# A fused attention and two MLPs: three blocks of tokens instead of two go uncombined through the first MLP, one weight matrix at a time

## The chip, the cores and the metric

The kernel runs on one core of a Trainium2 chip. The metric is the device time of one execution, in microseconds; of the kernel before three runs gave 1757.72, 1759.16 and 1761.06, median 1759.16. TensorE (PE) multiplies, VectorE (DVE) and ScalarE (ACT) do the elementwise work, and all transfers between DRAM and the on-chip memory are issued, in order, by SyncE (SP).

## The reference

```python
# q, k, v: (8, 8, 576, 64)
q_s = softmax of q over its last axis;  k_s = softmax of k over the sequence
kv = einsum('bhsd,bhse->bhde', k_s, v)
x  = einsum('bhsd,bhde->bhse', q_s, kv)      # -> (4608, 512)
h = x @ w_in                                 # (512, 2048)
r = maximum(h, 0);  x = (r * r) @ w_out      # (2048, 512)
gate = 1 / (1 + exp(-(x @ w_gate)))          # (512, 1536)
val = x @ w_val
return (gate * val) @ w_out2                 # (1536, 512)
```

The weights of both MLPs arrive as 64-bit floats.

## The kernel before

The 4608 tokens are nine blocks of 512 (0 to 8), four key tiles of 128 channels each. Every float32 product is made of three matmuls on high and low parts (`mm3`, L217 to 220: high by high, high by low, low by high), so everything that is multiplied is first split: ACT makes the high part (`hi_of`, L212), DVE subtracts it for the low part (`lo_of`, L215).

A raw weight tile is 128 x 512 numbers of 64 bits. `w_load` (L245) fetches it; ACT takes the words apart (L255, L261), DVE makes a 32-bit float of them in four instructions (L268, L269, L272, L279). The split of it, `whl`, is 0.5 MB, is written to a DRAM tensor (`w_store`, L297) and fetched again by later stages (`w_fetch`, L302, into `ws`).

Most stages use a Strassen-Winograd scheme with seven products in place of eight ("combined"). It needs sums of weight tiles (`w_comb`, L293) and of input tiles, and works on a pair of blocks; PE then multiplies 128 x 512 tiles. Four units of 84 matmuls make the first matrix of the first MLP for a pair; its second matrix takes 384 matmuls more, uncombined. The ninth block has no partner, so its two halves of 256 tokens are paired (`in_stage` with `nt` 256): the same 720 matmuls, with 256 columns each.

Blocks 0 and 1 go through the first MLP uncombined (`conv_stage`), 384 matmuls of 512 columns each: for each of 16 slices f of the hidden layer, 12 matmuls for the first matrix (`c_in`) into bank 4 or 5, relu and square on ACT (`c_g`), the split of that (`c_hi`, `c_lo`, tile `g0hl`), and 12 matmuls for the second matrix (`c_out`) into banks 0 to 3. In block 0 the weights are converted as they are needed, both matrices side by side, and the four sums of each group of the first matrix are made and split in the same stretch: 8 splits for each 4 raw tiles. Block 1 fetches the splits back. Then come the pairs (2, 3) and (4, 5) through the first MLP, (0, 1) and (2, 3) through the second, (6, 7) and the single block 8 through the first, and the rest through the second. The attention of later blocks is spread beside these stages.

The order of the instructions is set by `Plan`: every operation has a due time, engines it may run on, predecessors, and buffers it takes and gives back by tag. A list scheduler with fixed costs plays this through once and emits each engine's program in the order in which it would start. `plan.chain` forces an order on the weight fetches. On the chip only that order and the semaphores remain, and every engine, SP included, takes its instructions strictly in turn. Buffers are few: 10 of tag W (raw tiles, fetched splits), 14 of X, 19 of f, 5 of w.

Of the kernel before, what the change touches and what calls it, by code (L numbers as in the profile page):

```python
# [26 lines left out]
CHOSEN = object()  # L27
# [118 lines left out]
def attention_mlp_mlp(  # L146
# [158 lines left out]
    def plan_w(kind, g, T, dT, tag, conv, lead=6.0):  # L305

        N4 = [(kind, g, b) for b in range(4)]
        for b in range(4):
            t = conv[b] - 8 if conv else T + b * dT
            key = N4[b]  # L310
            add(t - lead, {DMA: 1.5}, ("wl",) + key, w_load, kind, g, b, tag, take=["W", tag] if wide else [tag])
            if wide:
                add(t, {ACT: 0.66}, ("wa",) + key, w_abs, key, tag, after=[("wl",) + key])
                add(t + 0.1, {ACT: 0.66}, ("wc",) + key, w_low, key, after=[("wl",) + key])
                add(t + 0.2, {DVE: (1.55, 2.05)}, ("wb",) + key, w_bits, key, after=[("wa",) + key])
                add(t + 0.4, ROUND, ("wr",) + key, w_round, key, CHOSEN, after=[("wb",) + key, ("wc",) + key], give=["W"])
        done = "wr" if wide else "wl"
        U = 4 * dT if not conv else 1.0
        t1 = (max(conv) - 4 if conv else T + U)

        def split(i, b, t, after, give=(), keep=None, store=True):
            key = (kind, g, i)
            htag = "X" if keep else "W"
            add(t, {ACT: 0.63}, ("wh",) + key, w_hi, key, b, htag, after=after, take=[htag])
            add(t + 0.2, LOW, ("wo",) + key, w_lo, key, b, CHOSEN, after=[("wh",) + key], give=give)
            if store:
                add(t + 1 if keep else t - 10, {DMA: 1.5}, ("ws",) + key, w_store, key, after=[("wo",) + key], give=[] if keep else ["W"])

        def comb(nm, o, a, b, op, t, after):
            add(t, VEC, ("wm", kind, g, nm), w_comb, kind, g, o, a, b, op, CHOSEN, after=after)  # L330

        D_ = [(done,) + x for x in N4]
        s = dT / 2 if not conv else 1.0

        ct = (lambda b: conv[b] - 5) if conv else (lambda b: t1)
        split(4, 3, ct(3), [D_[3]], keep=conv)
        split(1, 0, ct(0), [D_[0]], keep=conv)
        split(2, 1, ct(1), [D_[1]], keep=conv)
        s0 = []
        if conv or kind == "out":  # L340
            split(0, 2, ct(2), [D_[2]], keep=conv)
            s0 = [("wo", kind, g, 0)]
        M = lambda nm: ("wm", kind, g, nm)
        O = lambda i: ("wo", kind, g, i)
        if kind == "out":

            add(t1 + 9, {FREE: 0.0}, ("wfree", kind, g), lambda: None, after=[O(0), O(1), O(2), O(4)], give=[tag] * 4)
            return
        comb("S1", 3, 2, 3, ALU.add, t1 + s, [O(4), D_[2], *s0])
        comb("S3", 2, 0, 2, ALU.subtract, t1 + 2 * s, [M("S1"), D_[0], *s0])  # L350
        comb("S2", 0, 3, 0, ALU.subtract, t1 + 3 * s, [M("S3"), O(1)])
        comb("S4", 1, 1, 0, ALU.subtract, t1 + 4 * s, [M("S2"), O(2)])
        split(5, 3, t1 + 3 * s, [M("S1")])
        split(7, 2, t1 + 4 * s, [M("S3")], give=[tag])
        split(6, 0, t1 + 5 * s, [M("S2")])
        split(3, 1, t1 + 6 * s, [M("S4")], give=[tag])
        add(t1 + 7 * s, {FREE: 0.0}, ("wfree", kind, g), lambda: None, after=[O(5), O(6), O(3)], give=[tag] * 2)

# [90 lines left out]
    NPE = 2  # L449

# [121 lines left out]
    slack = lambda j: SLACK if j > 3 else 0.0  # L572
# [20 lines left out]
    def plan_q(j, p, key, step, qmul):  # L593
# [297 lines left out]
    for g in range(NU):  # L891
        for kind in ("in", "out"):
            plan_w(kind, g, 0, 0, "f", conv_times(kind, g))

    def conv_stage(j, T0, TS):

        ready = lambda kind, g, i: ("wo", kind, g, i) if j == 0 else ("wf", ("c", kind, g, i))
        kvs = [("kv", 0, p) for p in range(NP)]
        tag = "X" if j == 0 else "W"
        for f in range(F1):  # L900
            t = T0 + TS * f
            g, r = divmod(f // 2, 2)
            if j and f % 2 == 0:
                for kind, ii in (("in", ((1, 2), (0, 4))[r]), ("out", ((1, 0), (2, 4))[r])):
                    for i in ii:
                        plan_fetch((kind, g, i), c_use(j, kind, g, i), t - 14 + 3 * (kind == "out"))
            for kt in range(KT):
                i = (1, 2, 0, 4)[2 * r + kt // 2]
                if kt:
                    wait = [("ch", j, f, kt - 1)]  # L910
                elif f > 1:
                    wait = [("cg", j, f - 2)]
                else:
                    wait = kvs if j == 0 else [("cg", j - 1, F1 - 2 + f)]
                add(
                    t, {PE: 3 * MM}, ("ch", j, f, kt), c_in, j, f, kt,
                    after=[("x", j, kt), ready("in", g, i)] + wait, give=["SX"[j]] if f == F1 - 1 else [],
                )
                if f % 2 and kt % 2:
                    add(t, {FREE: 0.0}, ("cf", j, f, kt), lambda: None, after=[("ch", j, f, kt)] + ([("ws", "in", g, i)] if j == 0 else []), give=[tag])  # L920
            add(t + 2.6, {ACT: 1.24}, ("cg", j, f), c_g, f, after=[("ch", j, f, KT - 1)], take=["a"])
            add(t + 3.7, {ACT: 0.62}, ("chi", j, f), c_hi, f, after=[("cg", j, f)], take=["S"])
            add(t + 4.2, LOW, ("clo", j, f), c_lo, f, CHOSEN, after=[("chi", j, f)], give=["a"])
            ii = ((1, 0), (2, 4))[r]
            if f:
                wait = [("co", j, f - 1)]
            else:
                wait = kvs if j == 0 else [("cev", j - 1, o) for o in range(KT)]
            add(t + 6, {PE: 12 * MM}, ("co", j, f), c_out, j, f, after=[("clo", j, f)] + [ready("out", g, i) for i in ii] + wait, give=["S"])
            if f % 2:  # L930
                add(t, {FREE: 0.0}, ("cof", j, f), lambda: None, after=[("co", j, f)] + ([("ws", "out", g, i) for i in ii] if j == 0 else []), give=[tag, tag])
        t = T0 + TS * F1 + 6
        for o in range(KT):
            add(t, {ACT: 0.6} if o % 2 == 0 else {DVE: 0.7}, ("cev", j, o), c_ev, o, after=[("co", j, F1 - 1)], take=["a"])
            add(t + 1, {DMA: 0.8}, ("ost", j, o, 1), c_st, j, o, after=[("cev", j, o)], give=["a"])
        freed[0, 1] = (t + 1, [("cev", j, 0), ("cev", j, 1)])
        freed[2, 3] = (t + 2, [("cev", j, 2), ("cev", j, 3)])
        freed[4, 5] = (t - 4, [("cg", j, F1 - 2), ("cg", j, F1 - 1)])
# [63 lines left out]
    NPAIR = (NB - 1) // 2  # L1002
# [248 lines left out]
```

## Time and profile before

| | |
|---|---|
| median of three runs | 1759.16 us |
| span of the profiled execution | 1754.5 us |
| what lies around the span (median less span) | 4.7 us |
| PE busy | 1683.9 us, 96% |
| DVE, ACT busy | 1151.3 us, 926.1 us |
| moved by DMA | 443.27 MB, mean 253 GB/s |

The profiled execution's own total is not shown; the three runs stand for it. A busy PE is not PE at its peak: the mean granted clock was 0.978 over the span, and well below that in the first two hundred microseconds. A matmul row has the time from start to modelled end; matmuls overlap, so what one costs is the distance between starts.

### The profile page before, as it was taken

How to read it: one execution, taken by the hardware profiler on the slowest of the kernel's cores; microseconds unless marked ns; L12 is line 12 of the kernel's file. 1: busy time of each engine (PE TensorE's matmuls, PEld its weight loads, DVE VectorE, ACT ScalarE, POOL GpSimd, SP SyncE). 2: the span in 40 equal slices, each digit the busy share in tenths (PEclk: the TensorE clock that was granted, in tenths of full speed). 3: DMA queues.
4: the chain of work that ended last, by engine and by line, in shares of the span. 5: the costliest groups of instructions: out<-in, count | busy, mean ns of one | idle time of the engine just before them, and what ended most of it. 6: DMA issues, size and time to landing. Idle time of an engine off the chain costs nothing.

```text
span 1754.5 us, 25121 instructions
## 1 busy us (share of the span) xinstructions
PE 1683.9 (96%) x9124; PEld 1450.3 (83%) x9124; DVE 1151.3 (66%) x2192; ACT 926.1 (53%) x1711; POOL 2.1 (0%) x15
## 2 busy tenths in 40 slices
PE   5877899999989999999999999999999999999999
PEld 4655788788877887889988898888998899889999
DVE  7878877788776577568667685352364485447555
ACT  6776446666646575445457555271453354335344
POOL 0000000000000000000000000000000000000000
PEclk7888899999999999999999999999999999999999
DMA  7778777868778889985766566375777557655797
GB/s 277 269 281 284 257 240 262 308 234 300 266 286 311 315 287 346 346 290 182 248 209 210 177 215 213 105 254 190 287 283 285 192 187 245 204 194 191 226 376 274
DMA packets 149146, 443.27 MB, mean 253 GB/s; under 512 B 15648, under 2 KB 27936, under 8 KB 149024
## 3 DMA queue, kind: packets, MB, share of 16 engines
q1 hardware_dynamic: 149024, 441.68, 72.2%
q8 instruction: 72, 1.18, 0.3%
q14 instruction: 50, 0.41, 0.1%
HBM read 357.20 MB, written 84.41 MB: 252 GB/s over the span
## 4 chain that ended last, share of the span: by engine, by line
PE 79%; DMA 9%; DVE 7%; ACT 3%; issue 1%; SPq 1%; ACTq 0%; DVEq 0%
PE bank L218 25%; PE bank L219 25%; PE bank L220 25%; DMA wraw<-in_moe_w_out_dram 3%; PE xps L550 2%; DMA w_gv<-whl 2%; PE kps L427 1%; DMA w_in<-whl 1%; DMA wraw<-in_moe_w_val_dram 1%; DVE whl L215 1%; DVE wf L279 1%; DVE bX L215 1%; ACT wf L255 1%; DMA wraw<-in_moe_w_gate_dram 1%; DVE wf L272 1%
## 5 line engine op out<-in xcount | busy, mean ns | idle before, releaser
L218 PE MATMUL bank<-bX,ws 128*128 128x512 f32 (+1 forms) x1288 | 480.8, 373 | 8.2 <-DMA ws<-w_in 4.6
L219 PE MATMUL bank<-bX,ws 128*128 128x512 f32 (+1 forms) x1288 | 473.2, 367 | 0.0
L220 PE MATMUL bank<-bX,ws 128*128 128x512 f32 (+1 forms) x1288 | 472.9, 367 | 0.0
L709 DVE TENSOR_TENSOR s<-s,bank 128x512 f32<-128x512 f32 (+1 forms) x303 | 190.0, 632 | 217.8 <-PE bank L220 177.4
L218 PEld LDWEIGHTS bank<-bX,ws 128*128 128x128 f32 x1288 | 244.1, 189 | 48.2 <-DMA ws<-w_in 5.1
L212 ACT ACTIVATE s<-bank 128x512 f32<-128x512 f32 (+1 forms) x303 | 165.7, 554 | 223.2 <-PE bank L220 205.3
L220 PEld LDWEIGHTS bank<-bX,ws 128*128 128x128 f32 x1288 | 243.7, 189 | 40.9
L219 PEld LDWEIGHTS bank<-bX,ws 128*128 128x128 f32 x1288 | 244.1, 190 | 37.2 <-issue 0.5
L212 ACT ACTIVATE bS<-s 128x512 fp32r<-128x512 f32 (+1 forms) x306 | 175.5, 582 | 155.3 <-PE bank L220 136.2
L215 DVE TENSOR_TENSOR bS<-s,bS 128x512 fp32r<-128x512 f32 (+1 forms) x306 | 190.3, 632 | 82.1 <-ACT bS L212 75.1
L218 PE MATMUL bank<-ws,bS 128*128 128x256 f32 x756 | 214.5, 284 | 0.0
L219 PE MATMUL bank<-ws,bS 128*128 128x256 f32 x756 | 213.9, 283 | 0.0
L220 PE MATMUL bank<-ws,bS 128*128 128x256 f32 x756 | 213.9, 283 | 0.0
L218 PE MATMUL bank<-bS,ws 128*128 128x512 f32 (+1 forms) x512 | 188.4, 368 | 1.0 <-DMA ws<-w_out 0.7
L219 PE MATMUL bank<-bS,ws 128*128 128x512 f32 (+1 forms) x512 | 185.9, 363 | 1.4 <-DVE bS L215 1.4
L220 PE MATMUL bank<-bS,ws 128*128 128x512 f32 (+1 forms) x512 | 185.7, 363 | 0.0
L218 PEld LDWEIGHTS bank<-ws,bS 128*128 128x128 f32 x756 | 145.0, 192 | 0.8
L219 PEld LDWEIGHTS bank<-ws,bS 128*128 128x128 f32 x756 | 145.1, 192 | 0.7
L220 PEld LDWEIGHTS bank<-ws,bS 128*128 128x128 f32 x756 | 145.0, 192 | 0.0
L728 ACT ACTIVATE s<-s 128x512 f32<-128x512 f32 (+1 forms) x120 | 70.4, 588 | 130.7 <-DVE s L709 130.6
L218 PEld LDWEIGHTS bank<-bS,ws 128*128 128x128 f32 x512 | 96.7, 189 | 16.9 <-DMA ws<-w_out 1.1
L219 PEld LDWEIGHTS bank<-bS,ws 128*128 128x128 f32 x512 | 96.7, 189 | 16.6 <-DVE bS L215 1.6
(122 smaller groups left out, 2250.0 us busy)
## 6 DMA issues: line engine op xcount, KB each, us to landing
ws<-w_gv SPq DMA_DIRECT2D x210, 512.0 KB, 4.6
ws<-w_out SPq DMA_DIRECT2D x185, 512.0 KB, 4.2
ws<-w_in SPq DMA_DIRECT2D x128, 512.0 KB, 5.3
w_gv<-whl SPq DMA_DIRECT2D x42, 512.0 KB, 5.2
w_out<-whl SPq DMA_DIRECT2D x37, 512.0 KB, 5.2
w_in<-whl SPq DMA_DIRECT2D x32, 512.0 KB, 4.0
wraw<-in_moe_w_out_dram SPq DMA_DIRECT2D x28, 512.0 KB, 4.6
vt<-in_v_dram SPq DMA_DIRECT2D x32, 325.0 KB, 4.9
```

Source lines behind the costliest of these rows:

```text
L212: nc.scalar.activation(out=dst, in_=src, func=AF.Copy)
L215: by_name[engine].tensor_tensor(out=dst, in0=src, in1=hi.bitcast(F32), op=ALU.subtract)
L218: nc.tensor.matmul(ps, ah, bh, start=first, stop=False, skip_group_check=True)
L219: nc.tensor.matmul(ps, ah, bl, start=False, stop=False, skip_group_check=True)
L220: nc.tensor.matmul(ps, al, bh, start=False, stop=last, skip_group_check=True)
L255: nc.scalar.activation(out=t, in_=high.bitcast(F32), func=AF.Abs)
L272: nc.vector.scalar_tensor_tensor(out=w, in0=high, scalar=-0x40000000, in1=w, op0=ALU.bitwise_and, op1=ALU.bitwise_or)
L279: by_name[engine].tensor_tensor(out=w, in0=w, in1=low, op=ALU.add)
L427: nc.tensor.matmul(ps[:, 0:2 * D + 1], kt[:, r, :], vt[:, r, 0:2 * D + 1], start=(r == 0), stop=(r == RK - 1))
L550: nc.tensor.matmul(ps[:, e], kvf[b % 2][p], t[:, e], start=True, stop=True)
L709: nc.vector.tensor_tensor(out=t, in0=t, in1=banks[pr[b]][:, 0:n], op=ALU.add)
L728: nc.scalar.activation(out=t, in_=t, func=AF.Sigmoid)
```

## The change

Three blocks (0, 1, 2) go uncombined, and the pairs of the first MLP become (3, 4), (5, 6), (7, 8). The second MLP keeps its pairs and its half-block stage. The uncombined part is cut by matrix: the first matrix of block 0; then the first of block 1 beside the second of block 0, slice by slice; the first of block 2 beside the second of block 1; the second of block 2. Raw tiles of the first matrix are converted in the first of these stretches, those of the second matrix in the next. All raw tiles now use the 5 buffers of tag w in place of 19 of f, which hold the relu outputs waiting for their second matrix.

The four sums of a group are no longer made beside block 0. Each 32-bit tile of the first matrix is also written to DRAM (`w_store32`, 0.25 MB, 16 of them) and read back in the third stretch or later (`w_load32`), where sums and their splits are made. A tag-w buffer is given back when its split is made and that write has landed. A new chain, `worder`, fixes the order of all raw loads and read-backs.

```diff
+    def w_store32(key):
+        d = dp.tile([128, 512], F32, tag="w32_%s%d%d" % key, name="w32_%s%d%d" % key)
+        nc.sync.dma_start(out=d, in_=wf[key])
+        w32[key] = d
+
+    def w_load32(key, tag):
+        t = wf[key] = tile2(tag, "wf")
+        nc.sync.dma_start(out=t, in_=w32[key])
...
+    def plan_first(kind, g, times, tag):
+        for b in range(4) if kind == "in" else (0, 2, 1, 3):
+            t = times[b]
+            done = plan_raw(kind, g, b, t - 8, tag, 8.0)
+            i = SPLIT[b]
+            plan_split(kind, g, i, b, t - 5, t - 4, done, htag="X")
+            end = [("wo", kind, g, i)]
+            if kind == "in":
+                add(t - 3.9, {DMA: 0.8}, ("w32", kind, g, b), w_store32, (kind, g, b), after=done)
+                end.append(("w32", kind, g, b))
+            add(t - 3, {FREE: 0.0}, ("wfre", kind, g, b), lambda: None, after=end, give=[tag])
+
+    def plan_late(kind, g, T, s, tag):
+        ready = {}
+        for b in range(4):
+            add(T - 8, {DMA: 0.8}, ("wl32", kind, g, b), w_load32, (kind, g, b), tag, after=[("w32", kind, g, b)], take=[tag])
+            worder.append(("wl32", kind, g, b))
+            ready[b] = [("wl32", kind, g, b)]
+        plan_sums(kind, g, ready, {}, T, s, tag)
...
-    T0, TS = 27.0, 6.4
-    TC = F1 * 24 * MM * 1.06
-    T1 = T0 + TS * F1 + 8 + TC
+    T0, TS0, TS1 = 27.0, 4.4, 5.8
+    T2 = T0 + TS0 * F1
+    T3 = T2 + TS1 * F1
+    T4 = T3 + TS1 * F1
+    T1 = T4 + 2.9 * F1 + 4
...
+    for g in range(NU):
+        plan_first("in", g, [T0 + TS0 * (4 * g + 2 * (b // 2)) for b in range(4)], "w")
+    for g in range(NU):
+        plan_first("out", g, [T2 + TS1 * (4 * g + 2 * (b % 2)) + 3 for b in range(4)], "w")
+    for g in range(NU):
+        plan_late("in", g, T3 + 10 + 35 * g, 4.0, "w")
...
-    conv_stage(0, T0, TS)
-    conv_stage(1, T0 + TS * F1 + 1, TC / F1)
+    for f in range(F1):
+        conv_in(0, f, T0 + TS0 * f)
+    for j, T in ((1, T2), (2, T3)):
         for f in range(F1):
+            conv_in(j, f, T + TS1 * f)
+            conv_out(j - 1, f, T + TS1 * f + 3)
+    for f in range(F1):
+        conv_out(NONE - 1, f, T4 + 2.9 * f)
...
-    BLOCKS = [(2 * n, 2 * n + 1) for n in range(NPAIR)] + [(NB - 1,)]
+    IN = [tuple(range(j, j + 2)) for j in range(NONE, NB, 2)]
+    GATE = [(j, j + 1) for j in range(0, NB - 1, 2)] + [(NB - 1,)]
...
-    plan_blocks([1], T0 + 6, TS * F1 - 45)
-    plan_blocks(BLOCKS[1], T0 + TS * F1 - 25, (TC - 20) / 2)
-
-    BESIDE = {0: 2, 3: 3, 4: 4}
+    plan_blocks([1], T0 + 6, TS0 * F1 - 20)
+    plan_blocks([2], T2 + 6, TS1 * F1 - 30)
+    plan_blocks(IN[0], T3 + 5, (T1 - T3 - 40) / 2)
+
+    BESIDE = {0: 1, 3: 2}
...
-    for names in (fetched, xorder, sorder):
+    for names in (worder, fetched, xorder, sorder):
```

DVE, early in block 0, from the second relu output or the third weight tile on; `whl` is a weight split, `g0hl` the split of a relu output, `wf` a 32-bit tile. Before:

```order
L215 TENSOR_TENSOR whl<-wf,whl 128x512
L471 TENSOR_REDUCE qst<-qt 128x8
L417 TENSOR_TENSOR kt<-kt,kps 128x640
L500 TENSOR_SCALAR qst<-qst 128x8
L293 TENSOR_TENSOR wf<-wf 128x512
L215 TENSOR_TENSOR g0hl<-g_446,g0hl 128x512
L293 TENSOR_TENSOR wf<-wf 128x512
L268 TENSOR_SCALAR wf<-wf 128x512
L269 TENSOR_SCALAR wf<-wf 128x512
L272 SCALAR_TENSOR_TENSOR wf<-wraw,wf 128x512
```

In the changed kernel:

```order
L215 TENSOR_TENSOR whl<-wf,whl 128x512 x2
L443 TENSOR_TENSOR kt<-kt,kps 128x640
L530 TENSOR_SCALAR qst<-qst 128x8
L268 TENSOR_SCALAR wf<-wf 128x512
L269 TENSOR_SCALAR wf<-wf 128x512
L272 SCALAR_TENSOR_TENSOR wf<-wraw,wf 128x512
```

The sums (L293) and the splits of relu outputs (`g0hl`) have left this stretch; conversions and their own splits follow each other.

SP, from the first stores of block 0 on; `wraw` is a raw tile, `w_in` and `w_out` as a destination are the DRAM tensors. Before:

```order
L245 DMA wraw<-in_moe_w_in_dram 128x512 x2
L245 DMA wraw<-in_moe_w_out_dram 128x2x256 x2
L297 DMA w_in_384<-whl 128x1024
L297 DMA w_in_398<-whl 128x1024
L245 DMA wraw<-in_moe_w_in_dram 128x512
L459 DMA qt<-in_q_dram 128x512
L297 DMA w_out_435<-whl 128x1024
L245 DMA wraw<-in_moe_w_in_dram 128x512
```

In the changed kernel (L310 is the write of a 32-bit tile):

```order
L310 DMA w_in_336<-wf 128x512
L489 DMA qt<-in_q_dram 128x512
L310 DMA w_in_351<-wf 128x512
L297 DMA w_in_360<-whl 128x1024
L245 DMA wraw<-in_moe_w_in_dram 128x512
L297 DMA w_in_383<-whl 128x1024
L245 DMA wraw<-in_moe_w_in_dram 128x512
L310 DMA w_in_410<-wf 128x512
```

Twelve raw tiles stood ahead of the first store before; now five do, and the sixth and each later raw load stands behind writes of earlier tiles.

## Rows read from the trace of the kernel before

**Rows 1.** The page's slices (40 of 43.9 us): PE busy, granted clock, DMA.
```profile
PE   5877899999989999999999999999999999999999
PEclk7888899999999999999999999999999999999999
DMA  7778777868778889985766566375777557655797
```
**Rows 2.** Windows: length, busy us (instructions) by engine, granted clock, DMA share, GB/s.
```profile
37.80:205.00 167.20, 132.13 (x515) 99.33 (x515) 139.52 (x287) 112.83 (x241) 0.00 (x0) 0.84 0.77 271
37.80:312.00 274.20, 236.45 (x1016) 185.26 (x1016) 220.20 (x465) 170.60 (x345) 0.00 (x0) 0.90 0.77 269
205.00:312.00 107.00, 104.32 (x502) 85.92 (x501) 80.69 (x180) 57.78 (x105) 0.00 (x0) 0.99 0.77 265
312.00:360.00 48.00, 47.30 (x224) 39.11 (x224) 34.40 (x73) 33.80 (x63) 0.00 (x0) 0.99 0.90 312
1221.30:1316.00 94.70, 92.96 (x748) 91.32 (x747) 44.13 (x101) 48.28 (x122) 0.00 (x0) 1.00 0.76 289
1340.00:1400.00 60.00, 60.00 (x266) 49.73 (x265) 29.09 (x44) 21.55 (x36) 0.00 (x0) 1.00 0.63 212
```
**Rows 3.** Timeline of PE: start and end of the uncombined blocks.
```profile
37.86 0.78 PE L218 MATMUL bank<-x,whl 128*128 128x512 f32 x1
...
311.35 0.63 PE L220 MATMUL bank<-g0hl,ws 128*128 128x512 f32 x1
311.78 0.63 PE L218 MATMUL bank<-bX,ws 128*128 128x512 f32 x1
```
**Rows 4.** PE's groups, 880 to 980 us: count, busy, mean ns, idle before.
```profile
L218 PE MATMUL bank<-bX,ws 128*128 128x512 f32 x124 | 51.1, 412 | 0.0
L220 PE MATMUL bank<-bX,ws 128*128 128x512 f32 x125 | 48.9, 391 | 0.0
...
L427 PE MATMUL kps<-vt,kt 128*128 128x129 f32 x50 | 6.5, 276 | 0.0
```
**Rows 5.** DVE's groups, 37.5 to 205 us.
```profile
L215 DVE TENSOR_TENSOR whl<-wf,whl 128x512 fp32r<-128x512 f32 x46 | 30.6, 685 | 13.0 <-ACT whl L212 12.8
L272 DVE SCALAR_TENSOR_TENSOR wf<-wraw,wf 128x512 int32<-128x512 int32 x30 | 20.8, 693 | 1.0
L279 DVE CUSTOM_DVE_ANT_0 wf<-wraw,wf 128x1024 uint16<-128x1024 uint16 x31 | 20.4, 681 | 0.0
L269 DVE TENSOR_SCALAR wf<-wf 128x512 int32<-128x512 int32 x30 | 12.8, 427 | 1.0
L268 DVE TENSOR_SCALAR wf<-wf 128x512 f32<-128x512 f32 x30 | 12.6, 420 | 0.0
L293 DVE TENSOR_TENSOR wf<-wf 128x512 f32<-128x512 f32 x16 | 10.9, 682 | 0.0
```
**Rows 6.** ACT's groups, 37.5 to 205 us.
```profile
L212 ACT ACTIVATE whl<-wf 128x512 fp32r<-128x512 f32 x46 | 27.4, 622 | 26.2 <-DVE wf L279 14.6 <-DMA w_in<-whl 8.4 <-DVE qst L471 3.1
L255 ACT ACTIVATE wf<-wraw 128x512 f32<-128x512 f32 x24 | 15.7, 670 | 10.3 <-DMA wraw<-in_moe_w_out_dram 8.2 <-DMA wraw<-in_moe_w_in_dram 2.0
L510 ACT ACTIVATE qt<-qt,qst 128x64 f32<-128x64 f32 x32 | 8.0, 333 | 1.5 <-DVE qst L500 1.5
```
**Rows 7.** SP's waits, 36 to 205 us: total us, times, longest.
```profile
SPq L297 <- DVE whl L215: 38.5, 27, 4.8
SPq L297 <- DVE wf L268: 18.1, 8, 6.2
```
**Rows 8.** Timeline of DVE: last split of the first MLP's weights.
```profile
209.37 0.69 DVE L215 TENSOR_TENSOR whl<-wf,whl 128x512 fp32r<-128x512 f32 x1 [2.57 <-ACT whl L212]
```
**Rows 9.** Timeline of SP: last weight fetch of block 1.
```profile
292.69 0.32 SPq L302 DMA_DIRECT2D ws<-w_out  x1
```
**Rows 10.** DMA issues, 37.5 to 205 us: count, KB, median us to landing.
```profile
w_in<-whl SPq DMA_DIRECT2D x30, 512.0 KB, 4.0
wraw<-in_moe_w_in_dram SPq DMA_DIRECT2D x10, 512.0 KB, 5.0
```

More of the change, by code (lines that the diff above doesn't have):

```diff
@@ L303, in w_fetch @@
         whl[use] = t
[L305 to L342, printed above, removed]
@@ new lines, in attention_mlp_mlp, with plan_split @@
+    w32 = {}
+    worder = []
+    def w_store32(key):
[5 more added lines that the diff above has]
+        nc.sync.dma_start(out=t, in_=w32[key])
+    def plan_split(kind, g, i, b, t, ts, after, give=(), htag="W"):
+        key = (kind, g, i)
+        add(t, {ACT: 0.63}, ("wh",) + key, w_hi, key, b, htag, after=after, take=[htag])
+        add(t + 0.2, LOW, ("wo",) + key, w_lo, key, b, CHOSEN, after=[("wh",) + key], give=give)
+        add(ts, {DMA: 1.5}, ("ws",) + key, w_store, key, after=[("wo",) + key], give=[] if htag == "X" else ["W"])
@@ new lines, in plan_raw @@
+    def plan_raw(kind, g, b, t, tag, lead):
+        key = (kind, g, b)
+        add(t - lead, {DMA: 1.5}, ("wl",) + key, w_load, kind, g, b, tag, take=["W", tag] if wide else [tag])
+        worder.append(("wl",) + key)
+        if wide:
+            add(t, {ACT: 0.66}, ("wa",) + key, w_abs, key, tag, after=[("wl",) + key])
+            add(t + 0.1, {ACT: 0.66}, ("wc",) + key, w_low, key, after=[("wl",) + key])
+            add(t + 0.2, {DVE: (1.55, 2.05)}, ("wb",) + key, w_bits, key, after=[("wa",) + key])
+            add(t + 0.4, ROUND, ("wr",) + key, w_round, key, CHOSEN, after=[("wb",) + key, ("wc",) + key], give=["W"])
+        return [("wr" if wide else "wl",) + key]
@@ L343, in plan_w, with plan_sums @@
+    def plan_sums(kind, g, ready, own, t, s, tag):
         M = lambda nm: ("wm", kind, g, nm)
         O = lambda i: ("wo", kind, g, i)
[L345 to L357, printed above, removed]
+        def comb(nm, o, a, b, op, t, after):
+            add(t, VEC, M(nm), w_comb, kind, g, o, a, b, op, CHOSEN, after=after)
@@ L449, in attention_mlp_mlp @@
     NPE = 2
+    NONE = 3
+    XTAG = "SXX"
     JACT = 1
@@ L624, in plan_q @@
             kv_users[b, p].append(("xp",) + n)
-        if pe:
-            add(key + 8 * step, {ACT: 0.6}, ("xh",) + n, x_hi, j, p, after=[("xp",) + n], take=["SX"[j]])
+        if j < NONE:
+            add(key + 8 * step, {ACT: 0.6}, ("xh",) + n, x_hi, j, p, after=[("xp",) + n], take=[XTAG[j]])
             add(key + 9 * step, {DVE: 0.7}, ("x",) + n, x_lo, j, p, after=[("xh",) + n], give=["pa"])
@@ L891, in attention_mlp_mlp @@
     for g in range(NU):
[L892 to L899, printed above, removed]
-        for f in range(F1):
[L901 to L938, printed above, removed]
@@ L1081, in gate_stage @@
     def gate_stage(n, t):
-        js = BLOCKS[n]
+        js = GATE[n]
         nt = N if len(js) > 1 else N // 2
@@ L1087, in gate_stage @@
             for kt in range(KT):
-                add(t - 40, {DMA: 0.8}, ("xl", "x2", j, kt), x2_load, j, kt, after=([("ost", j, kt, 1)] if len(js) > 1 else [("ost", j, kt, 1, h) for h in range(2)]) + x_before["gate", n], take=["x"])
+                add(t - 40, {DMA: 0.8}, ("xl", "x2", j, kt), x2_load, j, kt, after=[("ost", j, kt, 1)] + x_before["gate", n], take=["x"])
         xn = ("X2", n)
```

112 lines of the change are left out of this document (86 added, 26 removed).

## Prediction

> **What bounds the kernel now.** I read the slices of the page first. PE is at nine tenths or more in nearly all of them, except the first five, where the granted clock is low as well [rows 1]. So nothing but PE's own work matters later, and the first 200 us are where a change of order can gain. The windows show it. From 37.8 to 205 us PE is busy 132.1 of 167.2 us at a granted clock of 0.84, from 205 to 312 us it is busy 104.3 of 107.0 us at 0.99 [rows 2]. The timeline gives the edges: the first weight matmul starts at 37.86, the last of block 1 ends its turn at 311.78, where the first combined one starts [rows 3].
>
> How much is lost there needs a price for a matmul. From 1340 to 1400 us PE does nothing but 512-column matmuls, 266 in 60 us: 0.2256 us each [rows 2]. Blocks 0 and 1 are 768 of them, 173.3 us. Attention beside them: from 880 to 980 us PE does 374 of these (three lines of 124 to 125) and 50 records of the key-value product [rows 4]; the 374 take 84.4 us, so 15.6 us are attention. A block of 512 tokens brings about one batch, which is 40 such records: 12.5 us. Between 37.8 and 312 us that is three blocks, 37.5 us. Of 274.2 us, 173.3 and 37.5 are work and 63 are lost, to idle time and to a low clock together.
>
> What PE waits for is the conversion of weights. DVE is busy 139.5 of the 167.2 us, 83%, ACT 67%, the DMA engines 77% [rows 2]. The largest groups of DVE are the four steps of a conversion, 0.42 + 0.43 + 0.69 + 0.68 = 2.22 us a tile, the splits at 0.69, and 16 sums [rows 5]. ACT waits 14.6 us of its split time for DVE's last conversion step, 8.4 us for a store that must free a buffer [rows 6], and SP's stores wait 38.5 us for DVE's splits [rows 7]. It is a round of small waits with DVE the fullest.
>
> **The change part by part.** *Matmuls.* The half-block stage goes. From 1221.3 to 1316 us PE ran 748 matmuls, the stage's 720 of 256 columns and 28 others of 512 [rows 2]; less 28 x 0.2256 = 6.3 us it takes 88.4 us. In its place block 2 costs 384 x 0.2256 = 86.6 us. As an exchange of work that is 2 us, nothing more.
>
> *Attention.* Before the end of the uncombined part block 4 now comes too (12.5 us), which stood beside a later stage. It is moved, not saved.
>
> So the new span is 1754.5 - 312.0 - 88.4 - 12.5 + E = 1341.6 + E, where E is the time at which the uncombined part ends. Everything after it has the same stages as before, all bound by PE; I take their seams as unchanged. E without any loss is 37.8 + 1152 x 0.2256 + 4 x 12.5 = 347.7 us. The question is what is lost on top, where 63 us were.
>
> *First stretch (first matrix of block 0).* PE's work is 192 x 0.2256 + 12.5 = 55.8 us; the conversions are slower. DVE has 14 tiles left to convert when the first split is done (31.1 us), 15 splits (10.3 us) and the attention of block 1. For that: busy 139.5, less 108.1 of the six groups of rows 5, less 14 relu splits (9.6), is 21.8 us for one and a half blocks, 15 for one. Rows overlap in a busy time, so this is a lower bound: 56 us or more. ACT has 11 tiles by two steps of 0.67 (14.7), 15 splits of 0.62 (9.3), 64 short exponentials and scalings of 0.333 for block 1 (21.3) [rows 6], and relu and square besides. The end is not before 98 us (60 us, DVE without a gap); at the 83% and 67% these engines reached, and with ACT now nearly as full as DVE, I take 78 us, an end at 116 us.
>
> *Second stretch (block 1's first matrix, block 0's second).* PE: 86.6 + 12.5 = 99.1 us. DVE by difference with the kernel before, which had its last split at 209.4 us [rows 8], 171.6 us after the start: 16 sums (10.9) and 16 splits (11.0) fewer, half a block of attention more (7 at least; I take 10). That gives 160 us, the last split at 198 us, and the two slices of PE that hang on it end at 209. From 116 us PE alone would end at 215; with 6% for waits, 221 us. The extra 16 writes of 0.25 MB lie under other work if the queue has room (below).
>
> *Third and fourth.* 576 x 0.2256 = 129.9 us and two blocks of attention, 25. The sums and their 16 splits (22 us of DVE), 16 read-backs and 16 stores are here, beside PE; conversions are not. Before, with conversions over, PE idled 2.7 of 107 us [rows 2]; I take 6% again, because more bytes go by: 164 us, E = 385.
>
> **Sum.** 1341.6 + 385 = 1726.6 us of span; the median of the runs lies 4.7 above the span shown, so 1731 us. Lost are 385 - 347.7 = 37 us instead of 63.
>
> *The queue.* Counting the transfers in SP's program, block 1's last weight fetch came after 78.2 MB and was issued at 292.7 us [rows 9], 267 GB/s from the start; 19 us later the part ended. Block 2's last fetch comes after 106.0 MB. My E wants it at 366 us, 290 GB/s. From 312 to 360 us the kernel moved 312 GB/s with PE busy 47.3 of 48.0 us [rows 2]. So the rate exists; it is not certain that waits of SP let it through.
>
> **Rivals.**
> (a) *Less is lost.* DVE runs without gaps (98 us) and the later stretches lose 3%: E = 98 + 254 x 1.03 = 360, 1706 us. For it: PE's 2.7 us of idling. Against it: DVE and ACT never ran that full over 60 us. 15%.
>
> (b) *The clock.* PE has 56 us of work in 78 us, with gaps after each pair of tiles. Low clock shows as starts 0.43 us apart, as at 311.35 and 311.78 [rows 3]. If the whole first stretch ran so, 192 x 0.43 = 82.6 us and attention at 1.7 times its price (21) make PE its bound: 104 us, E = 411, 1757 us. The granted clock of 0.84 between 37.8 and 205 us, in which PE idled 35 us, speaks for some of it, not for all. 10%. [...]
>
> (c) *The queue goes no faster than before.* 106.0 MB at 267 GB/s are there at 397 us, E = 416, 1762 us: no gain. Against it: that rate was kept down by waits for DVE [rows 7], which has less to do for each byte of the later stretches. 13%.
>
> (d) *The five buffers: slower.* All 32 raw loads go through five tiles instead of 19. A trip is: landing 5.0 [rows 10], ACT 1.3, DVE 2.2, landing of the 32-bit write 4.0 (as the split's), 12.5 us if nothing waits. 27 tiles follow the first five, so 5.4 trips; they fit into the 160 us of DVE's work up to 30 us a trip. But SP takes its instructions in turn: the load for a freed buffer stands behind the write and the split store of each of the five tiles, and a store's wait for DVE was up to 4.8 to 6.2 us [rows 7]. Five waits of 4.8 make 36.5 us a trip, 197 us, conversions end 37 us late, E = 422 and 1768 us. It decides from a trip of about 35 us on. For it: the sixth raw load stands behind three writes where twelve raw loads stood ahead of any. Against it: the waits are mostly for DVE's progress, which the estimate has already, and are not added five times. 10%. [...]
>
> That the change is not there is no rival: the order shows the stretches as described.
>
> **Numbers.** My forecast has 52%, (a) 15, (b) 10, (c) 13, (d) 10. Range 1708 to 1760: it takes in (b) and most of (a), leaves out (d), half of (c) and the best end of (a), less than 20% together. A measurement tells 0.2% (3.5 us) from no change. Faster than 1755.6: forecast, (a), about half of (b) and the low part of (c), 78%; within: 9%; slower: (d) and the rest of (c), 13%.
>
> **What would show it.** Right: first weight matmul still near 38 us; the last of block 0's first matrix near 116 us; block 1's and block 0's stretch ending near 221 us with DVE fullest until about 200; the first combined matmul near 385 us; no 256-column stage with `bX` before the last stage; later stages unchanged within a few us. Wrong in (b): starts 0.43 us apart through most of the first 80 us. Wrong in (c): DMA share near 0.9 or PE waiting for `ws` after 221 us. Wrong in (d): ACT waiting for raw tiles of 64 bits and DVE idle behind it, while SP waits at L310 or L245. The prediction is wrong as a whole if E is near 385 but the later stages take longer, since I gave them nothing.

## The result, and the profile after

The changed kernel takes 1714.16 us (median of four runs, 1711.9 to 1716.33), the kernel before 1758.61 us beside it (four runs): a ratio of 0.9754, 95% interval 0.9737 to 0.9772. That is 44.5 us less, where 28 were forecast. The profiled execution has a span of 1714.5 us and a time of 1716.33 us.

The page's slices of the changed kernel (42.9 us each; PE busy, granted clock, DMA), to be held against [rows 1]:

```profile
PE   5889999999999999999999999999999999999999
PEclk8989999999999999999999999999999999999999
DMA  6999878799787889799757555755576557655797
```

Two weak slices are left of four after the first. The windows, with the columns of [rows 2], cut where the stretches end; below them one that lies inside the first stretch:

```profile
38.00:117.00 79.00, 68.13 (x283) 50.10 (x284) 66.09 (x147) 67.03 (x160) 0.00 (x0) 0.91 0.92 326
117.00:214.00 97.00, 97.00 (x460) 80.48 (x459) 79.74 (x165) 64.04 (x114) 0.00 (x0) 1.00 0.90 323
214.00:378.00 164.00, 158.79 (x753) 131.06 (x752) 109.75 (x233) 83.22 (x149) 0.00 (x0) 0.99 0.78 271
60.00:80.00 20.00, 16.91 (x77) 11.94 (x77) 18.72 (x44) 19.81 (x51) 0.00 (x0) 1.00 0.94 357
```

In the second stretch DVE still works 82% of the time and converts as before, but PE is busy for all of its 97.00 us. In the first, DVE (84%) and ACT (85%) are both nearly full. The queue carries 326 and 323 GB/s where it carried 271.

The edges, from PE's timeline (start, us, line, operation), as in [rows 3]: the last matmul of the first stretch, the last of the second (of block 0's second matrix), the first combined one, and the last uncombined one.

```profile
116.86 0.39 PE L220 MATMUL bank<-x,whl 128*128 128x512 f32 x1
...
214.34 0.39 PE L220 MATMUL bank<-g0hl,whl 128*128 128x512 f32 x1
...
374.86 0.39 PE L218 MATMUL bank<-bX,ws 128*128 128x512 f32 x1
...
378.72 0.39 PE L220 MATMUL bank<-g0hl,ws 128*128 128x512 f32 x1
```

The ends overlap: six combined matmuls start before the last uncombined one. So that all kernels can be compared, E is from here on the start of the last uncombined matmul, plus its 0.23 us, less 0.2256 us for each combined one ahead of it, and the rest is span less E. The kernel before has E = 314.9 and 1439.6 behind it, the changed kernel 377.6 and 1336.9. To lay them beside each other I give the kernel before a third uncombined block at its price (86.6 + 12.5, so E = 414.0) and take its half-block stage and batch (88.4 + 12.5) off the rest: 1338.7. The 40.0 us between the two spans are then 36.4 in the uncombined part, 1.8 in the exchange of work, and 1.8 in all that follows.

What DVE and ACT do in the first stretch (38 to 117 us; groups as in [rows 5] and [rows 6]):

```profile
L272 DVE SCALAR_TENSOR_TENSOR wf<-wraw,wf 128x512 int32<-128x512 int32 x17 | 11.8, 693 | 0.6
L279 DVE CUSTOM_DVE_ANT_0 wf<-wraw,wf 128x1024 uint16<-128x1024 uint16 x16 | 10.4, 685 | 0.0
L215 DVE TENSOR_TENSOR whl<-wf,whl 128x512 fp32r<-128x512 f32 x15 | 9.8, 682 | 0.6 <-ACT whl L212 0.6
...
L215 DVE TENSOR_TENSOR x<-xps,x 128x512 fp32r<-128x512 f32 x5 | 3.4, 689 | 5.4 <-ACT x L212 5.4
```
```profile
L255 ACT ACTIVATE wf<-wraw 128x512 f32<-128x512 f32 x14 | 8.8, 662 | 4.3 <-DMA wraw<-in_moe_w_in_dram 4.3
L212 ACT ACTIVATE whl<-wf 128x512 fp32r<-128x512 f32 x15 | 8.8, 617 | 0.0
```

The 15 splits cost what they cost before; DVE's wait for ACT ahead of them was 0.6 us, where it had been 12.8 us ahead of 46 splits, and ACT has no idle time ahead of its own. SP's waits in the same stretch (total, times, longest), for [rows 7]:

```profile
SPq L310 <- DVE wf L279: 21.2, 13, 4.3
SPq L297 <- DVE whl L215: 12.6, 9, 4.0
```

The last splits of the first MLP's weights on DVE, for [rows 8], and the last issue of a weight of the second matrix to the uncombined part, for [rows 9]:

```profile
198.28 1.29 DVE L215 TENSOR_TENSOR whl<-wf,whl 128x512 fp32r<-128x512 f32 x2 [1.56 <-ACT whl L212]
```
```profile
364.79 0.32 SPq L302 DMA_DIRECT2D ws<-w_out  x1
```

A store of a split lands 4.3 us after its issue, 4.0 before [rows 10].

### The profile page after: what moved, and what is told of

The parts are those of the page before. It is cut to its first block, busy times and chain, and to the rows that moved or that the text cites. A ratio compares the mean times of both kernels' runs of the same rounds, so it can differ in the third digit from the quotient of the medians.

```text
span 1714.5 us, 24259 instructions
## 1 busy us (share of the span) xinstructions
PE 1666.9 (97%) x8788; PEld 1425.3 (83%) x8788; DVE 1127.2 (66%) x2109; ACT 916.4 (53%) x1649; POOL 2.1 (0%) x15
## 4 chain that ended last, share of the span: by engine, by line
PE 85%; DMA 7%; DVE 4%; ACT 2%; issue 1%; SPq 1%; ACTq 0%; DVEq 0%
PE bank L218 27%; PE bank L220 27%; PE bank L219 27%; PE xps L580 2%; PE kps L453 1%; DMA qt<-in_q_dram 1%; DMA ws<-w_in 1%; DMA wraw<-in_moe_w_gate_dram 1%; DMA wraw<-in_moe_w_out_dram 1%; DMA vt<-in_v_dram 1%; DMA ws<-w_gv 1%; DVE whl L215 0%; PE qsw L511 0%; PE bank L453 0%; ACT wf L255 0%
## 5 line engine op out<-in xcount | busy, mean ns | idle before, releaser
L218 PE MATMUL bank<-bX,ws 128*128 128x512 f32 (+1 forms) x1176 | 446.3, 379 | 7.2 <-DMA ws<-w_in 5.7
L220 PE MATMUL bank<-bX,ws 128*128 128x512 f32 (+1 forms) x1176 | 440.7, 375 | 0.0
L219 PE MATMUL bank<-bX,ws 128*128 128x512 f32 (+1 forms) x1176 | 440.7, 375 | 0.0
L739 DVE TENSOR_TENSOR s<-s,bank 128x512 f32<-128x512 f32 (+1 forms) x279 | 179.9, 651 | 215.4 <-PE bank L220 178.4
L212 ACT ACTIVATE s<-bank 128x512 f32<-128x512 f32 (+1 forms) x279 | 156.7, 568 | 215.4 <-PE bank L220 213.7
L218 PEld LDWEIGHTS bank<-bX,ws 128*128 128x128 f32 x1176 | 222.0, 189 | 47.5 <-DMA ws<-w_in 4.7
L220 PEld LDWEIGHTS bank<-bX,ws 128*128 128x128 f32 x1176 | 221.7, 189 | 40.3
L219 PEld LDWEIGHTS bank<-bX,ws 128*128 128x128 f32 x1176 | 222.1, 189 | 37.7 <-issue 0.5
L212 ACT ACTIVATE bS<-s 128x512 fp32r<-128x512 f32 (+1 forms) x282 | 166.1, 597 | 147.1 <-PE bank L220 129.7
L215 DVE TENSOR_TENSOR bS<-s,bS 128x512 fp32r<-128x512 f32 (+1 forms) x282 | 180.9, 650 | 75.2 <-ACT bS L212 67.7
L218 PE MATMUL bank<-ws,bS 128*128 128x256 f32 x756 | 214.6, 284 | 0.0
L218 PE MATMUL bank<-bS,ws 128*128 128x512 f32 x384 | 150.5, 392 | 0.0
L220 PE MATMUL bank<-bS,ws 128*128 128x512 f32 x384 | 149.5, 389 | 0.0
L219 PE MATMUL bank<-bS,ws 128*128 128x512 f32 x384 | 149.5, 389 | 0.0
L212 ACT ACTIVATE whl<-wf 128x512 fp32r<-128x512 f32 x111 | 68.0, 624 | 42.2 <-PE bank L220 12.0
L215 DVE TENSOR_TENSOR whl<-wf,whl 128x512 fp32r<-128x512 f32 x111 | 74.1, 685 | 20.3 <-ACT whl L212 19.3
```

The costliest lines, as they stand in the source:

```text
L212: nc.scalar.activation(out=dst, in_=src, func=AF.Copy)
L215: by_name[engine].tensor_tensor(out=dst, in0=src, in1=hi.bitcast(F32), op=ALU.subtract)
L218: nc.tensor.matmul(ps, ah, bh, start=first, stop=False, skip_group_check=True)
L219: nc.tensor.matmul(ps, ah, bl, start=False, stop=False, skip_group_check=True)
L220: nc.tensor.matmul(ps, al, bh, start=False, stop=last, skip_group_check=True)
L739: nc.vector.tensor_tensor(out=t, in0=t, in1=banks[pr[b]][:, 0:n], op=ALU.add)
```

## The experiments

All were timed beside the kernel before, whose medians were 1755.8 to 1757.8 us there (1758.61 beside the changed kernel); each ratio is to that. In the table, stretch 1 is the start of the last matmul of the first matrix of block 0; E and the rest are as defined above, those of `before` and `two` with the exchange taken into account, so that columns compare. E and the rest come from one profiled execution of each kernel. For `side_late`, `again_jact`, `paced_jact` and `three` that was the fastest one, 6.6, 7.9, 4.5 and 2.5 us under the median.

| kernel | median us | ratio, interval | stretch 1 | E | rest |
|---|---|---|---|---|---|
| before | 1758.61 | 1 | 196.6 | 414.0 | 1338.7 |
| changed | 1714.16 | 0.9754 (0.9737, 0.9772) | 116.9 | 377.6 | 1336.9 |
| `three` | 1750.68 | 0.998 (0.9964, 0.9995) | 194.7 | 411.3 | 1335.1 |
| `two` | 1742.17 | 0.9924 (0.9897, 0.9951) | 112.3 | 377.2 | 1361.9 |
| `side_late` | 1750.53 | 0.9961 (0.9943, 0.9979) | 173.1 | 404.1 | 1338.1 |
| `ring8` | 1719.75 | 0.9786 (0.9764, 0.9808) | 113.5 | 389.9 | 1328.3 |
| `ring4` | 1735.27 | 0.9871 (0.9851, 0.9891) | 117.9 | 379.8 | 1353.4 |
| `jact` | 1715.23 | 0.9763 (0.9744, 0.9782) | 112.8 | 376.6 | 1335.6 |
| `early8` | 1721.0 | 0.9792 (0.9772, 0.9813) | 133.6 | 392.7 | 1328.9 |
| `held` | 1731.64 | 0.9859 (0.9829, 0.989) | 115.9 | 368.2 | 1364.1 |
| `again` | 1739.07 | 0.99 (0.9868, 0.9931) | 114.1 | 401.3 | 1336.5 |
| `again_jact` | 1742.78 | 0.9921 (0.9898, 0.9944) | 113.6 | 399.9 | 1333.2 |
| `paced` | 1733.6 | 0.9868 (0.985, 0.9886) | 117.2 | 397.1 | 1335.8 |
| `paced_jact` | 1718.07 | 0.978 (0.9761, 0.9799) | 115.3 | 376.1 | 1335.2 |

The theories: A, the gain is the cut by matrix; B, it is the exchange of the half-block stage for a third uncombined block; C, it is that the sums leave the first stretch.

### One part of the change at a time

**`three`**: the kernel before with the third block uncombined, both matrices side by side and the sums beside block 0 as before.

```diff
+    NONE = 3
...
+    conv_stage(2, T0 + TS * F1 + 1 + TC, TC / F1)
...
+    IN = [tuple(range(j, j + 2)) for j in range(NONE, NB, 2)]
```

> Third block uncombined and pairs (3,4), (5,6), (7,8), but both matrices of block 0 converted side by side and their sums beside it, as before. Theory A (conversions must be hidden under matmuls of another block): block 0's part is as it was, the uncombined part ends at 312.0 + 86.6 + 12.5 = 411 us, total 1752 to 1760 us. Theory B (the gain is the half-block stage replaced by block 2): 1712 to 1725 us.

It is 0.2% faster, 1.3 us under A's range, and its uncombined part ends where A put it (411.3 us); B falls. The first 205 us are as in [rows 2]:

```profile
36.00:205.00 169.00, 132.16 (x517) 99.21 (x516) 140.33 (x286) 110.23 (x235) 0.00 (x0) 0.85 0.76 273
```

**`two`**: the changed kernel with two uncombined blocks: cut by matrix, late sums, and the half-block stage back.

```diff
-    NONE = 3
+    NONE = 2
...
-        plan_late("in", g, T3 + 10 + 35 * g, 4.0, "w")
+        plan_late("in", g, T2 + 45 + 25 * g, 4.0, "w")
...
-    for j, T in ((1, T2), (2, T3)):
+    for j, T in ((1, T2),):
```

> Two blocks uncombined, cut by matrix, sums late from the copy in DRAM; block 8 goes by halves through the first MLP, as before. Theory A: about 30 us lost in the uncombined part instead of 63, the part ends near 279 us, total 1715 to 1732 us. Theory B: without the third block nothing is gained, 1750 to 1762 us.

A miss: 1742.17. The uncombined part gained what the whole change gains there (36.8 us), and 23.2 came back behind it. The windows on either side of its first combined matmul (261.7), and what PE waited for from 223 to 600 us (total, times, longest):

```profile
223.00:262.00 39.00, 34.39 (x159) 28.32 (x158) 29.86 (x59) 18.16 (x34) 0.00 (x0) 0.96 0.78 269
262.00:310.00 48.00, 35.42 (x143) 28.23 (x142) 39.92 (x76) 24.78 (x45) 0.00 (x0) 0.82 0.84 300
```
```profile
PE bank L218 <- DMA ws<-w_in: 15.1, 5, 6.1
```
And DVE's timeline: the last group of sums, whose splits the combined stage fetches, is still being made when it has begun. Below it is the longest of PE's waits, for a fetch of such a split.

```profile
276.29 0.69 DVE L293 TENSOR_TENSOR wf<-wf 128x512 f32<-128x512 f32 x1 [3.22 <-DMA wf<-w_in]
...
282.19 0.68 DVE L293 TENSOR_TENSOR wf<-wf 128x512 f32<-128x512 f32 x1
...
299.90 0.80 PE L218 MATMUL bank<-bX,ws 128*128 128x512 f32 x1 [6.07 <-DMA ws<-w_in]
```

So the third block has a worth that the exchange of work does not show: its 164 us of matmuls cover the late sums. (In the changed kernel the first read-back is issued at 180.4 us and the first sum starts at 209.2, so this begins in the second stretch.)

**`side_late`**: three blocks, late sums, both matrices side by side in each block (8 buffers of tag w, 16 of f).

```diff
+    TS0 = 6.4
...
-    for f in range(F1):
-        conv_in(0, f, T0 + TS0 * f)
-    for j, T in ((1, T2), (2, T3)):
+    for j, T, ts in ((0, T0, TS0), (1, T2, TS1), (2, T3, TS1)):
...
-            conv_out(j - 1, f, T + TS1 * f + 3)
+            conv_out(j, f, T + ts * f + 6)
```

> Third block uncombined and sums late from the copy in DRAM, but block 0's two matrices converted side by side and every block finished before the next (8 buffers of tag w, 16 of f). Theory A: DVE is spared 22 us of sums and splits, but 32 tiles are still converted under one block's matmuls: 1730 to 1745 us. Theory C (the gain is the sums made later): 1710 to 1722 us.

1750.53, so C falls, and A's range was missed by 5.5 us. Without the sums block 0 is through its second matrix at 183.5 us instead of 214.7; two thirds of that are lost again by the end of the part. In the next two blocks PE idles 10.8 us at a clock of 0.97 and 0.98; the first of them:

```profile
184.00:300.00 116.00, 108.27 (x499) 87.77 (x498) 65.75 (x138) 52.29 (x93) 0.00 (x0) 0.97 0.79 273
```

By medians, each beside its own runs of the kernel before, the exchange gives 5.1 us, exchange and late sums together 5.3, cut and late sums without the exchange 13.6; all three 44.5. Cut and exchange without the late sums are `early8` below (with eight buffers), and they give 36.8. So A is right in that nothing gives much without the cut, and most of the gain does not need the late sums. Whether the cut alone, with two blocks and early sums, would be enough was not tried: `two` has the late sums too, and PE's waits for their splits are a part of what comes back there.

### What bounds the first stretch

PE has 56 us of work in its 79. **`ring8`** and **`ring4`** give the raw tiles eight and four buffers in place of five.

```diff
-    SIZES = {"X": 14, "W": 10, "S": 6, "f": 19, ..., "w": 5, ...}
+    SIZES = {"X": 14, "W": 10, "S": 6, "f": 16, ..., "w": 8, ...}
...
-    ytag = ["f"] * 19 + ["w"] * 5
+    ytag = ["f"] * 16 + ["w"] * 8
```

> The changed kernel with 8 buffers of tag w and 16 of f (it has 5 and 19). Theory of the five buffers: SP runs ahead by three more raw tiles, DMA between 20 and 40 us rises from 144 to 200 GB/s or more, the first stretch ends 5 to 10 us before 117, total 1703 to 1710 us. If DVE and ACT bound the first stretch: within 3 us of the changed kernel's 1714.

> The changed kernel with 4 buffers of tag w and 20 of f. Theory of the five buffers (a trip of 35 us with five): a trip serves a fifth fewer tiles, conversions of 32 tiles end 25 to 35 us later, total 1735 to 1750 us. If a trip is short (12 to 20 us) and DVE and ACT bound: up to 5 us slower, 1714 to 1720 us.

With eight the start is fuller, yet the stretch ends only 3.4 us earlier, so five are not what mainly bounds it; the third and fourth lose more than that:

```profile
20.00:40.00 20.00, 12.48 (x39) 8.20 (x39) 15.78 (x37) 14.12 (x27) 0.00 (x0) 0.62 0.63 228
...
214.00:378.00 164.00, 149.37 (x687) 123.00 (x686) 101.10 (x218) 78.57 (x141) 0.00 (x0) 0.95 0.78 270
```

The changed kernel moved 144 GB/s in the first of these windows. With four buffers the first two stretches end within 1.0 us of the changed kernel's. Its total fits what the theory of the five buffers said, but not for its reason: the loss is 16.5 us in the rest, where tag w serves the second MLP's raw tiles, and PE waits there for a weight split (378 to 1720 us):

```profile
PE bank L218 <- DMA ws<-w_gv: 10.7, 1, 10.7
```

**`jact`** does block 1's softmax on DVE where the changed kernel has it on ACT, since ACT is as full as DVE.

```diff
-    JACT = 1
+    JACT = -1
```

> The changed kernel, but the softmax of block 1 subtracts and multiplies on DVE as the other blocks do, instead of 64 short instructions on ACT (21 us of ACT less, some 5 us of DVE more, all in the first stretch). If ACT bounds the first stretch: it ends 5 to 10 us earlier, 1704 to 1710 us. If DVE bounds it: 3 to 6 us later, 1717 to 1720 us. If the five buffers do: no change.

ACT's busy time falls by 9.4 us, DVE's rises by 3.1, the stretch ends 4.0 us earlier, and the total is the same within the runs. PE's busy time is lower and its clock higher, so a part of these 4 us may be clock; no run separates the two:

```profile
38.00:117.00 79.00, 65.91 (x295) 48.56 (x294) 69.16 (x148) 57.65 (x106) 0.00 (x0) 0.98 0.93 332
```

**`early8`** is `ring8` with the sums back in the first stretch and no 32-bit copy.

```diff
+            own = {b: [("wo", kind, g, SPLIT[b])] for b in range(4)}
+            plan_sums(kind, g, ready, own, max(times) - 3, 1.0, tag)
...
-    for g in range(NU):
-        plan_late("in", g, T3 + 10 + 35 * g, 4.0, "w")
```

> As ring8 (8 buffers of w), but the sums of the first matrix and their splits made beside block 0 from the tiles on the chip; nothing is written or read back as 32-bit copy (8.4 MB less). If DVE's work in the first stretch decides: 22 us more of it, the stretch ends 15 to 22 us later than in ring8, total 12 to 20 us above ring8. If the copy's traffic is the dearer part: not above ring8.

The first stretch ends 20.1 us later than in `ring8`; the sums and their splits are 22 us of DVE. That is what DVE's work would do if it set this end nearly one for one, when it is added; but 16 more splits of ACT came with it, and PE's clock was 0.81, so the cause is not shown alone. The total was a miss: 1721.0, level with `ring8`, because the last stretches are then almost without loss:

```profile
38.00:117.00 79.00, 61.65 (x233) 46.12 (x234) 68.09 (x145) 61.75 (x145) 0.00 (x0) 0.81 0.79 290
...
235.00:399.00 164.00, 162.88 (x783) 135.56 (x783) 102.24 (x223) 79.83 (x141) 0.00 (x0) 1.00 0.70 242
```

With eight buffers the late sums take 20 us out of the first stretch and 3 out of E: what they free there comes back almost whole in the later stretches. Early sums with five buffers were not tried.

**`again`** drops the copy in DRAM: the raw tiles of the first matrix are loaded and converted a second time for the late sums. **`again_jact`** adds `jact`.

```diff
-            if kind == "in":
-                add(t - 3.9, {DMA: 0.8}, ("w32", kind, g, b), w_store32, (kind, g, b), after=done)
...
-            add(T - 8, {DMA: 0.8}, ("wl32", kind, g, b), w_load32, (kind, g, b), tag, after=[("w32", kind, g, b)], take=[tag])
+        ready = {b: plan_raw(kind, g, b, T + 1.0 * b, tag, 8.0, "again") for b in range(4)}
```

> The changed kernel without the 32-bit copy in DRAM: the raw tiles of the first matrix are loaded and converted a second time in the third stretch (35 us of DVE more there, 4.2 MB of writes less in the first stretch, bytes of the third stretch 4.2 MB more). If the queue bounds the first stretch (DMA share 0.92 there): 4.2 MB at 326 GB/s less, its end moves from 117 to 104 to 110 us. If DVE and ACT bound it: 114 to 119 us. The third stretch has room on DVE (110 of 164 us busy): total 1704 to 1714 us in the first case, 1712 to 1722 in the second.

> The kernel without the 32-bit copy, and block 1's softmax on DVE as other blocks have it (21 us of ACT less). If queue and ACT bounded the first stretch together, both relieved: its end at 98 to 106 us, total 1698 to 1710 us. If DVE is the next bound at once: as the kernel without the copy, or up to 5 us later.

Both missed. Without the 16 writes the first stretch ends 2.8 us earlier at a DMA share of 0.85, so the queue is not its bound. Nor do ring, ACT and queue add up: with queue and ACT relieved it ends at 113.6, with ACT alone at 112.8. Each of the three takes 3 to 4 us, and the end stays near 113; what holds it there the runs don't settle. Most of the total is lost to one wait of PE (214 to 405 us), 17.2 us in `again_jact`:

```profile
PE kps L419 <- DVE kmx L414: 15.9, 1, 15.9
```

### The cover of the third block, and the order in PE's queue

**`held`** keeps the read-backs of the 32-bit tiles back until late matmuls of the third and fourth stretches are done.

```diff
-            add(T - 8, ..., after=[("w32", kind, g, b)], take=[tag])
+            add(T - 8, ..., after=[("w32", kind, g, b), (("co", 1, 15), ("co", 2, 2), ("co", 2, 11), ("co", 2, 15))[g]], take=[tag])
```

> The changed kernel, but the read-back of the four groups' 32-bit tiles waits for slices near the end of the uncombined part (the last of block 1's second matrix, then slices 2, 11 and 15 of block 2's), so the sums stand as close to the first combined stage as in the kernel with two blocks. If the third block's worth is the cover it gives to the late sums: the uncombined part ends as before within 5 us, then PE waits 10 us or more for fetched splits, total 1724 to 1740 us. If the loss in the kernel with two blocks had another cause: 1710 to 1718 us.

The total is as expected, and the uncombined part is now 9.4 us shorter, with PE busy for all of 164 us; 27.2 us come back behind it. The way was another than expected: PE did not stand at fetched splits (2.0 us). The windows and PE's waits from 370 to 500 us:

```profile
214.00:378.00 164.00, 164.00 (x792) 137.07 (x790) 101.79 (x215) 78.11 (x138) 0.00 (x0) 1.00 0.74 258
378.00:440.00 62.00, 38.59 (x162) 31.02 (x161) 51.82 (x106) 42.55 (x76) 0.00 (x0) 0.78 0.91 331
```
```profile
PE xps L580 <- ACT whl L212: 15.1, 1, 15.1
```
The wait is put down to a split on ACT that ended at the same moment. But L580 reads `qtr`, and the transposition on DVE that writes it ended at 410.40, 0.15 us before PE went on. In DVE's timeline the last steps of that softmax stand behind conversions of the second MLP's raw tiles, and then behind one more conversion and the four sums of these tiles (L293):

```profile
401.48 0.69 DVE L557 TENSOR_TENSOR qt<-qt,qst 128x512 f32<-128x512 f32 x1
...
405.48 0.69 DVE L293 TENSOR_TENSOR wf<-wf 128x512 f32<-128x512 f32 x1
...
409.09 0.69 DVE L293 TENSOR_TENSOR wf<-wf 128x512 f32<-128x512 f32 x1
409.69 0.71 DVE L561 STREAM_TRANSPOSE qtr<-qt 128x512 f32<-128x512 f32 x1
```

In the changed kernel the same four sums run from 375.0 us on, 30 us earlier. Here DVE converts the first raw tile of the second MLP from 383.79 us on, between the last late sums (333.11 in the changed kernel). So in both kernels DVE's work has slid past the seam, where little uncombined work is left for PE: in `two` the late sums themselves, in `held` the second MLP's conversions behind them.

**`paced`** sets the due times of the three stretches to the measured pace; **`paced_jact`** the pace without the later first slice, with `jact`. Nothing else differs. The edit of `paced`:

```diff
-    T0, TS0, TS1 = 27.0, 4.4, 5.8
+    T0, TS0, TS1 = 37.0, 4.9, 6.1
```

> Only the due times of the three uncombined stretches change, to the pace that the changed kernel's trace shows (first slice due at 37 us, 4.9 us a slice in the first stretch, 6.1 in the middle ones). Theory P (the misses of ring8, early8, held and again came from instructions standing in PE's and ACT's queues in an order planned for a faster pace than the chip keeps): first stretch still near 117, second near 214, third and fourth 160 to 163 us, later stages 2 to 8 us shorter, total 1703 to 1712. Rival Q (the order is near its best as it is, and what the other kernels lost was their own): total 1711 to 1722, with one wait of over 4 us on PE somewhere that the changed kernel does not have.

> The paces 4.9 and 6.1 us a slice with the first slice due at 27 us as in the changed kernel, and block 1's softmax on DVE in place of ACT as in jact. Theory P: first stretch ends near 113, second near 210, total 1700 to 1710. Rival Q: the first stretch ends near 113 and the total is 1711 to 1725 all the same, as with jact (1715.2).

P falls, twice, and Q's range for `paced` was missed as well, by 12 us, though the new long wait that Q named is there. `paced` is 19 us slower than the changed kernel, and its first two stretches and its rest are the same; all of it is in the third and fourth. The timeline around the wait, PE and DVE:

```profile
362.54 0.39 PE L220 MATMUL bank<-g0hl,ws 128*128 128x512 f32 x1
...
373.18 0.68 DVE L215 TENSOR_TENSOR bX<-xf,bX 128x512 fp32r<-128x512 f32 x1
373.78 0.68 DVE L677 TENSOR_TENSOR xf<-xf 128x512 f32<-128x512 f32 x1
374.38 0.68 DVE L215 TENSOR_TENSOR bX<-xf,bX 128x512 fp32r<-128x512 f32 x1
374.98 0.41 DVE L417 TENSOR_TENSOR kmx<-kt 128x256 f32<-128x256 f32 x1
...
376.11 0.47 PE L425 MATMUL kps<-ident,kmx 128*128 128x128 f32 x1 [13.18 <-DVE kmx L420]
378.13 0.77 PE L218 MATMUL bank<-g0hl,ws 128*128 128x512 f32 x1 [1.55 <-DMA ws<-w_out]
```

DVE prepares the first combined stage without a pause (`xf`, `bX`, splits), and the maximum over the keys of the next attention batch stands behind that. In PE's program the small transpose of it stands ahead of uncombined matmuls that run only after it. In the changed kernel DVE comes to that maximum later still, yet nothing waits, because the transpose stands behind the seam:

```profile
390.19 0.43 DVE L417 TENSOR_TENSOR kmx<-kt 128x256 f32<-128x256 f32 x1 [0.84 <-DMA kt<-in_k_dram]
```

The waits of 15.9 and 17.2 us in `again` and `again_jact` name the same pair of instructions. This is read from the traces; no run moved that transpose alone. No version here beats the changed kernel; `jact` and `paced_jact` lie 1 and 4 us above it, `jact` within the spread of the runs. Why `ring8` loses in its third stretch stays open: its longest waits there are 5.3, 3.0 and 2.9 us, all at attention.

## Why the prediction was right, and where its sizes were off

The direction, the place and the mechanism held: the conversions of the second matrix now lie under another block's matmuls, and the later stages kept their time. The 17.1 us between 1731.3 and 1714.2 are four terms.

- *First stretch, 116 us*: measured 116.9 (at its end, 117.1). DVE was busy for 66.1 us of the window shown. Three of its 17 conversions there (6.7 us) were already for the second matrix; the other 59.4 us are the 60 that the step counted for DVE without a gap. That these would fill 77% of the stretch was a choice between the 83% and the 67% of before, and it came out. The step also took the 64 short instructions of ACT at their mean of 0.333 us (21.3 us), though such rows overlap: 32 of them kept ACT busy for 8.0 us [rows 6], so 64 are some 16.
- *Second stretch, end at 221*: the largest miss among the steps. It took the 215 us at which PE alone would end and charged 6% for waits, with no row behind the 6%. PE lost nothing, and the stretch ended at 214.6. DVE's last split was forecast for 198 and ended at 199.6. 6.4 us.
- *Third and fourth, 164 us*: measured 163.0 (377.6 - 214.6). 1.0 us, with the second stretch 7.4.
- *The edge*: 312.0 was subtracted as the end of the old uncombined part, but the first combined matmul ran ahead of twelve others; by the same rule as above it is 314.9. 2.9 us.
- *"Seams unchanged"*: right within 1.8 us, by which the rest was shorter.
- *4.7 us around the span*: a mistake of method. It set the median of some executions against the span of another. Where both are listed, the time of an execution is 1.7 to 3.0 us above its own span, 1.8 in the median and in the changed kernel's profiled one (1716.33 and 1714.5), so the execution profiled before took some 1756.3, by estimate. The changed kernel's profiled execution was in turn the slowest of its four, 2.2 us over their median, so that the term came out as -0.3. 5.0 us.

The rivals. (a) was half right: its first stretch of 98 us did not come, but its 3% on the 254 us that follow did (377.6 - 117.1 = 260.5, 2.6%). (b) fell: the granted clock was 0.91 between 38 and 117 us, and 1.00 in each 5 us from 45 to 85 and from 95 to 110 us, though PE was idle for 10.87 of the 79 us. Of 172 distances between the starts of `bank<-x,whl` matmuls that follow each other there, 112 are 0.22 to 0.24 us and 24 are the 0.42 to 0.43 us that (b) wanted throughout. Its 1.7 for attention was an estimate of mine that no row shows. (c) fell: 326 and 323 GB/s against its 267, and the last fetch of the second matrix was issued at 364.8 us where the forecast needed 366. So the old rate was no limit of the queue. (d) fell: SP did wait for DVE at its stores, 21.2 us at L310 alone, but the waits did not add up to PE's; with eight buffers the first two stretches end 3.4 and 2.8 us earlier.

What the prediction did not see is that its parts depend on each other. It priced the exchange at 2 us and the late sums as work "beside PE". `three` shows the exchange to be worth little without the cut, `early8` that cut and exchange together, with eight buffers, are worth 36.8 us without the late sums, and `two` and `held` what it costs when DVE's work slides past that cover: 23 and 27 us of the rest.

## What to carry to other kernels

Where weights must be prepared before the first use, order the work so that one operand's preparation lies under matmuls that need only what is ready, and don't charge those matmuls the waits of the old order: in the second stretch PE was busy for all of 97.00 us. Vector work that was moved later was cheap here only while independent matmuls stood beside it (past them `two` gave back 23.2 us and `held` 27.2); read what will stand there, and what comes right behind, and compare totals: with eight buffers the stretch that the sums left gained 20 us and the uncombined part 3. After any reordering look for one long wait before many small ones: at one small attention matmul that stood a few places too early in its order PE waited 13.18 us (`paced`), 15.9 (`again`) and 17.2 (`again_jact`), about a third of the whole gain.

## What the runs showed that I had not expected

- The transfers went beyond the highest rate that I had used (312 GB/s): 357 GB/s in a window of 20 us above, and in the changed kernel from 378 to 420 us, with PE busy for 40.16 of 42 us:

```profile
378.00:420.00 42.00, 40.16 (x186) 32.79 (x185) 34.66 (x69) 30.83 (x55) 0.00 (x0) 1.00 1.02 390
```

- PE's granted clock was 0.98 in `jact` against 0.91 in the same 79 us of the changed kernel, though PE was busy for less of them (65.91 us against 68.13); in `paced_jact`, with 68.40 us, it was 0.92. What decides it was not tried.
- Runs of one variant differ by 4.1 us (`paced`) to 10.7 us (`side_late`, 1743.95 to 1754.61), so among the best kernels here differences under some 4 us can't be told from none.
